# All keys and MLP rows turned by TensorE, none by transposing transfers, with a new order of operations

## The chip, the cores and the metric

One core of one Trainium2 chip runs the whole program in one launch. The time is the device time of one execution in microseconds (us). Below, PE is TensorE, DVE is VectorE, ACT is ScalarE, POOL is GpSimd and SP is the engine that here only issues transfers.

## The reference

The first half is a linear attention with a decaying state, over batch 4, 8 heads, 768 steps and a head size of 48; the second half mixes its output by a two-dimensional Fourier transform and sends it through a layer norm and an MLP from 384 to 1536 and back.

```python
for t in range(S):                                   # S = 768, D = 48
    cur = np.einsum('bhd,bhe->bhde', u[None] * kt, vt)
    y[:, :, t] = np.einsum('bhd,bhde->bhe', rt, state + cur)
    state = w[None, :, :, None] * state + np.einsum('bhd,bhe->bhde', kt, vt)
...
x = attn_out.transpose(0, 2, 1, 3).reshape(B, S, H * D)      # 4 x 768 x 384
mixed = np.real(np.fft.fft(np.fft.fft(x, axis=1), axis=2))
u = x + mixed
un = (u - mean(u)) / np.sqrt(var(u) + 1e-06)
out = u + np.maximum(un @ w_ch1, 0.0) @ w_ch2
```

Inputs r, k, v, w, u, w_ch1, w_ch2 and the output are float32.

## The kernel before

**Attention.** The sequence of each batch is cut into 6 chunks of 128 steps, 24 chunks in all (`NC`). `load` fetches k, r and v of a chunk through SP's queue. `attend` scales keys and queries by tables of the decay on DVE (`KR`, a tile of 128 steps by keys and queries of 4 pairs of heads, each padded to 128 columns) and casts v (`V`). Scores need keys and queries with the head dimension on partitions (`KRT`). For batch 0 the queries are turned once ahead of everything (`queries`, `QT6`) and the keys by 4 transposes for each chunk. For the 18 chunks of batches 1 to 3, `KRT` can be made in three ways: 8 transposes on PE into one PSUM bank (`tp`), copied out by ACT or by DVE, or one transposing transfer on SP's queue from `KR` (`xbar8`, line 468). In the kernel before, 8 of the 18 chunks take PE and 10 the transfer. Then follow the scores (line 493), the mask (`AC` on ACT with `MA` on POOL, or `MA` on DVE alone), the bonus term (`PR`, `de`, `DE`, `TT`), the carried state (`u`, `S`, `qs`) and the product with V (`y`, `X`).

**Fourier stage.** For each batch the rows are folded by symmetry (`EO`, `HH`, `XF`), then come two stages of matmuls (`fp` with `TT2` and its reversal `TR`, then `mp`), the sum `UF` with the attention's output, the centred rows `UB` and their statistics (`st`, `MV`, `rstd`).

**MLP.** The 768 rows of a batch are handled in two halves of 384, eight halves in all. The rows of a half must be turned (`UNT`), so that the model dimension is on partitions. Halves 0 and 1 do that on PE in 3 blocks (`turned`: 3 transposes, then a copy out of PSUM by DVE or ACT); halves 2 to 7 (`XBAR_HALVES`) by one transposing transfer each on SP's queue (`xbar9`, line 753). `mlp1` makes 12 tiles of 3 matmuls (line 773) with the ReLU on ACT or DVE (`HT`); `mlp2` makes 3 row blocks of 12 matmuls (line 793), a scale and sum on DVE (`osb`) and a store. W1 and W2 come by three transfers each on POOL's queue (lines 819 and 821); W2 lies in the tile that `queries` used at the start.

**What sets the order.** All operations are recorded first, each with its alternatives (engine and function), and are then emitted in an order that is written out as a list of numbers, `ORDER`. In it `468.1` is operation 468 in its second alternative, and `@4,2` names the PSUM banks it gets. Each engine runs its instructions in that order. `idle` emits a filler matmul on a tile of zeros that nothing reads; the list has 38 of them, all ahead of the first MLP matmul. Waits between engines come from the dependencies, and tiles are taken from rings in the order of emission (6 tiles of `kr`, `vt` and `KR`, 4 of `KRT`, 3 of `UNT`, 2 of `UB`).

Of the kernel before, what the change touches and what calls it, by code (L numbers as in the profile page):

```python
# [27 lines left out]
XBAR_HALVES = frozenset(range(2, 8))  # L28
# [69 lines left out]
211 182.1 188 150 173 151 157 227 171 159 180 155 176.1 229 208 160 187.1 169 167 178 168 231 174.1 158 152@0 161 181  # L98
153 185 156 205 172.1 184 170 162 179 177.1 154 165 163 233 186.1 164 235 215.1 189 196 197 200 212 201 175 216 198
218 166 199 214 190 228 213 192 295 0@1 1@1 2@1 3@1 4@1 5@1 6@1 7@1 8@1 9.1@1 219@1 194 221@2 230 217 297@3 220 313  # L100
225@4 332 315@5 222 232 223@6 351 334@7 226 298.1 353@0 316.1 236 378 224 335 299.2 317.1 10@1 11@1 12@1 13@1 14.2@1
300@1,2 303.1 234 318@5,4 319.1 193 207 210 304.1 307@6 321 301.1 380@3 237 325@1 296 322 320.1 302.1 326 308 314 15@5
16.1@5 17.2@5 305@5 239 306.1 354.1 327 355.2 18@4 19@4 20@4 356@4,2 359.1 202 333 240 309 323 360.1 363@0 328 203 357
206 310.1 248 381 324 311 352.2 364 337@4,2 340.1 336.2 312.1 358 382.2 195 238 21@7 22.2@7 383@7,6 365 341.1 344@3
379 342 345 384 386.1 338.1 390@4 249 405 329.1 330 191 346 407@6 391 242 408 209 392 343 243 183 387.1 361@5 366
362.1 339.1 385 367.1 241 347 368 409.2 331.1 388 393 430 369.1 348.1 293 349 394.1 350.1 245 370 395 389.1 371
410@7,2 413.1 411.1 250 432@6 372.1 414.1 406 415@1 412.1 396.1 244 416 204 23@0 24@0 25@0 418 417.1 373 26@0 27.1@0
419.1 486 420 433 374 28@0 29@0 30.2@0 488@0 376 397 431 246 398 421.1 448 31@2 32.2@2 440@3 489 294 400 33@2 34.1@2
450@5 399 251 377 491@7,4 404 451 375 247 422 811@2 403 823@6 423 492 424 453@1,0 254 402 441.1 425 815@5 401 428 816
449 427 812 429 819@4 426 456 820 434 821 255 813 467 824 825 814 817 822 457 826.1 252 35.1@1 36.2@1 435@1,2 438.1  # L110
487 493 439.1 469@4 818 253 442@6 1062 468 827 829@1 452 494 436.1 830.1 828 257 458 443 454 460@5 437.1 841@7 444 470
842.1 459 463 269 1061 445.1 524 861@0 831.1 867@2 1063 258 477 843.1 490 855@4 856 505 862.1 461 868.1 446 498@1 478
462 507.1@7 857 863.1 832 844 835@0 836 495 526.1@3 508.1 499 447.1 455 501 858 496@4 837 464.1 500 869.1 527.1
510@6,7 511.1 465 513 849@0 509 875@2 502.1 838 512.1 528.1 503 517@3 466.1 851@6 850 853@7 504.1 876 529@5,0 497 870
472@2,1 473.1 854 532 520 852 879@7 474.1 518 506.2 880.1 256 471.1 864 37.2@5 515 534@6 1067@5 1089@1 270 514 530.1
531.1 475 833 1068.1 1069@7 1090 859 519 521 479@0 266 1083@2 1070 834 480 877@5 533 535 516.1 522 1081@1 260 481.1
1084 1077@7 476 878.1 482 483 261 537 525 1065 541 484 1109@4 536 538 267 1079@2 1110 1131@5 1078 542.1 1125@4 1064
539 557 559.2 1129@7 485 560.2 871 1071@0 523 1072 540 263 1075@3 1132 544 1073@0 1130 545 546 1121@6 547 543 1127@5
1122 550 1117@7 632 1082 1123@6 1080 1118 548 1085@1 551 264 1074 549 1087@2 1124 552 1111@7 1128 553 272 575 1126
634@0 1086 1115@6 1076 554 1119@5 262 1088 561.1 577.1@4 259 1066 555 556 273 1112.1 881@1 882 1120.1 883 893@3 894  # L120
265 613 615.2 895 885@2 578.1 635 884 889@0 896 890 891 886 887 616.2 1097@7 888 839 562@5,1 892 580@3,4 897 563 1098
898 860 1116 1113@2 594 596.2 583 899@0 900 920@1 921 1114 579 597.2 569@6 901 581 1091@3 922 570 926@2 927 582 911@0
912 840 268 905@4 906 564 913 932@1 933 1092 558.2 928 565 584 1103@0 845 576 907 587@2 923 566 567@5 1104 846 568 847
571 572 1139@4 902 1105 588 908 651 653.2 585 590 1099 586.1 848 589 591 934 573 1100 914 872 574 617.1 1106 595 919
935 592 1107 604 1093 636.1 593 618@1,6 271 605 1094 621 274 1101 1140 929 622 654.2 1095 625@0 637@2,5 626 619 638.1
598.1 599@1,7 628 614 1145@3 1096.1 600 644@6 627 629 1141 280 940 620 640.1 639.1 602.1 641.1 603.1 623@5 1151@7
624.1 606@2 601 1161@1 1152.1 607 633 275 630 608 915 1146 645 652 631 1163@7 646 1162.1 647 648 281 642 1164 865
1167@0 668.1 643 656@1,7 649 276 669 659 657.1 609 610 655 1173@5 1168 650 660 611 1147 278 866 671 661@1 1171@0 612
662 1174 663 1102.1 664 665 658.1 1153@6 282 1155@2 1108 674 670 284 1201@5 675 1156 666 873 1193@7 1154 667 1165@2
1194 672 285 1207@6 676 1202 673 1195@1 1166 677 679 1208 1159@7 678 287 680 1169@5 681 1133@2 1170 683 279 1142 1160  # L130
682 1172 1134 903 1196 684 686.2 941@6 942 943 949@5 1148 944 721 723.2 687.2 945@7 703 946 1211@0 740 742.2 953@1
1135 288 1212.1 950 951 724.2 1136 952 702 704.2 947 954 955 948 1203@6 874 743.2 1143 956 1209@0 1149 1213@5 688 277
689@7,4 957 958.1 1204 1199@1 290 904 916 759 761.2 1210 1157@3 692 291 1197@6 1200 725.1 1137 1214 980@0 981 959@7
960 1198 286 982 992@1 993 693 1158 696@2 961 1181@5 690 283 994 965@6 966 697 962 691 909 726@0,3 745@7,4 746.1 748.1
685.2 1138.1 729 910 986@1 987 747.1 1144.1 1182 698 699 705.2 924 971@0 972 727 744.1 694@4 967 1183 695.1 988 1175@3
1150 983.1 989 733@6 712 700 749.1 734 1187@1 741.2 995 973 722.2 1176 713.1 1000 730 701 752@7 1188 968 735 1177 974
1189 917 778 780.2 753 979 731 1178 1184 732 754 936 762.2 707@0,2 736 737 706 710 755 756 1190 918 925 937 708 1185
1287@4 781.2 1179 709 1277@0 1191 714@2 728 1215@5 715 289 757 716 1299@3 1216 1186.1 758 717 718 292 1235@1 795.1
1180.1 738 750@5 1236.1 1278 1288 1300 1192.1 796.1 1291@7 739 764@0,4 765.1 711 783@3,1 784.1 766.1 767 786.1 1205@6
763.1 751.1 719 1253@0 720 760 1245@4 801.1 1254.1 1206 1251@2 975 1285@6 785.1 768 1252 769 771@0 1257@2 782 772 1246  # L140
770 773 1247@1 779 963 788@4 1258 774 775 791 964 1229@5 802 789 1292 787.1 790 792 1279@2 976 776 1297@7 1280 777
1248 793 984 1239@3 1298 797.1 794 1217@2 1286.1 1281@0 798.1 1237@1 800 1289@7 799 803 1249@4 805.1 1290 1230 1238
1283@6 1240 806 804 1295@7 807 1218 809 1296 808 1231 810 1243@1 1250.1 1001@3 1002 1284.1 1005@7 1006 1007 1244.1
1013@4 1003 1014 985 969 1015 1009@6 1232 1004.1 1016 1010 1008.1 1011 1223@1 1012 930 1219 1282 931 1017 1241@4 1018
1019@3 1020 1255@7 1021 1025@6 1026 1022.1 1031@0 1032 1027 1220 1033 1224 1028 1046@3 1047 1034.1 938 1242 1225 970
939 1023 1039 1256 1265@6 1024 1233 1052@0 1053 1226 1221 1234 1040@4 1041 1035 1301@7 1227 1271@5 990 1228.1 1266
1036 991 1222.1 1029 1259@2 996 1272 997 1042 1260 998 1030 1267 1054 1261 1044 1339@1 1048 1302 1050 1329@4 1056
1319@0 1045 1273 1320.1 1330 1043 1293@3 977 1051 1055.1 1049 1323@4 1294.1 1331@0 1060 1340.1 1324 1303 1057 1058
1335@3 1262 1336.1 1321@4 978 1274 1268 1313@1 1269 1325@3 1275 1270.1 1304 1263 1333@6 1276 1327@5 1264.1 1334 1383@2
1037 1322 1361@6 1307@4 1362.1 1384 1337@2 999 1326.1 1363@6 1338 1305 1365@3 1332.1 1308 1306 1373@2 1379@7 1314  # L150
1380.1 1371@0 1366.1 1377@7 1364.1 1349@3 1328.1 1309 1038 1369@6 1315 1370 1367@5 1374 1378 1341@6 1350 1342.1 1381@2
1375@7 1382 1355@6 1368 1372 1397@2 1356 1343@5 1310 1351 1311 1385@0 1376.1 1312.1 1316 1352 1317 1357 1353 1318.1
1398 1344 1354 1358 1399 1359 1345 1360.1 1391@4 1346 1392 1347 1386 1059 1348.1 1400 1387 1401 1393 1388 1402 1394
1389 1395 1390.1 1396.1
"""


def _order():
    out = []
    for tok in ORDER.split():  # L160
        tok, _, banks = tok.partition("@")
        n, _, a = tok.partition(".")
        out.append((int(n), int(a or 0), [int(x) for x in banks.split(",")] if banks else []))
    return out
# [3 lines left out]
def kernel(  # L168
# [11 lines left out]
    nc = tc.nc  # L180
# [8 lines left out]
    op = sch.op  # L189
# [20 lines left out]
    ident = const([128, 128], BF16, "ident")  # L210
# [441 lines left out]
    def fourier(b):  # L652
# [90 lines left out]
        for sh in range(2):  # L743
# [12 lines left out]
            else:  # L756
                for j in range(3):
                    turned(sh, j, UB, UNT)
# [102 lines left out]
```

## Time and profile before

| | |
|---|---|
| median of 3 runs | 174.62 us (173.65 to 176.54) |
| profiled execution | 176.04 us, span of its instructions 174.3 us |
| granted TensorE clock | 0.997 |
| busy PE, DVE, ACT, POOL | 160.1, 139.9, 104.5, 71.1 us |
| packets of the DMA queue that SP feeds | 89568, 22.19 MB, 65.4% of 16 engines' span |
| transposing transfers | 10 of keys and queries, 6 of MLP rows |

Rows of groups in the profile read: line, engine, operation, tiles written and read, shape and count, then busy time, mean duration in ns, and the idle time of the engine just before them with what ended it. Matmuls are pipelined: the duration of one is its latency, and the distance between starts in the timeline is what it takes of PE. Rows of waits read: who waited, for whom, us in total, how often, the longest.

### The profile page before, as it was taken

How to read it: one execution, taken by the hardware profiler on the slowest of the kernel's cores; microseconds unless marked ns; L12 is line 12 of the kernel's file. 1: busy time of each engine (PE TensorE's matmuls, PEld its weight loads, DVE VectorE, ACT ScalarE, POOL GpSimd, SP SyncE). 2: the span in 40 equal slices, each digit the busy share in tenths (PEclk: the TensorE clock that was granted, in tenths of full speed). 3: DMA queues.
4: the chain of work that ended last, by engine and by line, in shares of the span. 5: the costliest groups of instructions: out<-in, count | busy, mean ns of one | idle time of the engine just before them, and what ended most of it. 6: DMA issues, size and time to landing. Idle time of an engine off the chain costs nothing.

```text
span 174.3 us, 4274 instructions
## 1 busy us (share of the span) xinstructions
PE 160.1 (92%) x1595; PEld 110.8 (64%) x1595; DVE 139.9 (80%) x351; ACT 104.5 (60%) x248; POOL 71.1 (41%) x106
## 2 busy tenths in 40 slices
PE   4888798789999999999999998899999999999991
PEld 1384574578676787677666765567687666666550
DVE  6498999999988998889899899569989975441632
ACT  4968999799984986685657884566433050423000
POOL 8605760178962125997300596876200001100110
PEclk9999999999999999999999999999999999999998
DMA  5999798999999999999999899870001604210323
GB/s 139 289 202 207 152 220 208 239 188 212 207 168 204 172 133 220 130 209 217 230 223 154 187 246 244 120 201 4 0 0 30 177 8 104 95 45 0 125 101 137
DMA packets 91558, 26.79 MB, mean 154 GB/s; under 512 B 86977, under 2 KB 90178, under 8 KB 91538
## 3 DMA queue, kind: packets, MB, share of 16 engines
q1 hardware_dynamic: 89568, 22.19, 65.4%
q0 software_dynamic: 1440, 3.74, 10.1%
q10 hardware_dynamic: 530, 0.59, 0.9%
q8 instruction: 12, 0.20, 0.5%
q14 instruction: 8, 0.07, 0.1%
HBM read 19.77 MB, written 4.72 MB: 140 GB/s over the span
## 4 chain that ended last, share of the span: by engine, by line
PE 58%; DMA 14%; DVE 12%; issue 5%; POOL 5%; ACT 3%; SPq 1%; DVEq 0%; ACTq 0%; POOLq 0%
PE bank L773 22%; PE bank L793 21%; DMA W<-in_moe_w_ch_dram 5%; DMA HT<-in_r_dram 3%; PE bank L661 3%; DMA KRT<-KR 3%; DMA kr<-in_r_dram 3%; PE bank L700 2%; POOL TT L566 2%; PE bank L493 2%; PE bank L578 2%; DVE HH L609 2%; DVE MA L505 2%; PE bank L384 1%; DVE KR L424 1%
## 5 line engine op out<-in xcount | busy, mean ns | idle before, releaser
L773 PE MATMUL bank<-early,W 128*128 128x384 bf16 x288 | 55.0, 327 | 0.3 <-DMA W<-in_moe_w_ch_dram 0.2
L793 PE MATMUL bank<-W,HT 128*128 128x384 bf16 x288 | 54.4, 326 | 0.0
L778 ACT ACTIVATE HT<-bank 128x384 bf16<-128x384 f32 x71 | 31.1, 501 | 24.7 <-PE bank L773 24.7
L773 PEld LDWEIGHTS <-W 128*128 128x128 bf16 x288 | 30.8, 114 | 13.2 <-DMA W<-in_moe_w_ch_dram 0.5
L793 PEld LDWEIGHTS <-HT 128*128 128x128 bf16 x288 | 26.8, 98 | 14.7
L566 POOL TENSOR_TENSOR TT<-V,DE 128x384 bf16<-128x384 bf16 x22 | 19.9, 913 | 7.7 <-ACT DE L565 4.0
L502 POOL TENSOR_SCALAR_AFFINE_SELECT MA<-AC 128x512 bf16<-128x512 bf16 x25 | 16.4, 670 | 14.8 <-ACT AC L500 10.6
L800 DVE SCALAR_TENSOR_TENSOR osb<-bank,rstd,UF 128x384 f32<-128x384 f32 x24 | 13.9, 610 | 9.7 <-PE bank L793 9.6
L804 POOL DMA_DIRECT2D out_dram<-osb x7 | 3.9, 556 | 43.2 <-DVE osb L800 43.2
L424 DVE TENSOR_TENSOR KR<-kr,wtab 128x768 bf16<-128x768 f32 x18 | 18.8, 1051 | 0.9 <-DMA kr<-in_r_dram 0.9
L779 DVE TENSOR_SCALAR HT<-bank 128x384 bf16<-128x384 f32 x25 | 13.2, 550 | 7.6 <-PE bank L773 6.9
L478 POOL TENSOR_TENSOR PR<-KRT 128x512 bf16<-128x512 bf16 x9 | 10.4, 1166 | 20.3 <-DMA KRT<-KR 20.2
L500 ACT CAST AC<-bank 128x512 bf16<-128x512 f32 x25 | 14.6, 594 | 6.5 <-PE bank L493 4.2
L505 DVE TENSOR_TENSOR MA<-bank,mtri 128x512 bf16<-128x512 f32 x23 | 15.0, 677 | 0.7 <-PE bank L493 0.6
L719 ACT ACTIVATE UB<-UF,sm 128x384 bf16<-128x384 f32 x20 | 12.0, 614 | 3.3 <-DVE UF L712 3.2
L726 DVE BATCH_NORM_STATS2 st<-UF 128x6 f32<-128x384 f32 x24 | 12.9, 546 | 0.0
L586 DVE TENSOR_TENSOR X<-bank,TT 128x384 bf16<-128x384 f32 x15 | 8.3, 550 | 4.7 <-PE bank L578 4.7
L661 PE MATMUL bank<-te_t,XF 128*128 128x193 bf16 x96 | 10.4, 248 | 0.8 <-DVE XF L624 0.8
L284 PE MATMUL bank<-zero 128*128 128x512 bf16 (+2 forms) x38 | 10.5, 398 | 0.6 <-DVE PR L481 0.5
L712 DVE SCALAR_TENSOR_TENSOR UF<-bank,X 128x384 f32<-128x384 f32 x20 | 10.5, 545 | 0.7 <-PE bank L700 0.7
L669 ACT CAST TT<-bank 97x386 bf16<-97x386 f32 x13 | 7.3, 600 | 6.2 <-PE bank L661 6.1
L661 PEld LDWEIGHTS <-XF 128*128 128x128 bf16 x96 | 8.0, 98 | 2.8 <-DVE XF L624 1.4
(113 smaller groups left out, 256.1 us busy)
## 6 DMA issues: line engine op xcount, KB each, us to landing
kr<-in_k_dram SPq DMA_DIRECT2D x24, 192.0 KB, 4.3
vt<-in_v_dram SPq DMA_DIRECT2D x24, 192.0 KB, 4.1
kr<-in_r_dram SPq DMA_DIRECT2D x18, 192.0 KB, 4.6
out_dram<-osb SPq DMA_DIRECT2D x17, 192.0 KB, 2.1
W<-in_moe_w_ch_dram POOLq DMA_DIRECT2D x6, 384.0 KB, 6.1
out_dram<-osb POOLq DMA_DIRECT2D x7, 192.0 KB, 2.3
te_t<-te_c SPq DMA_DIRECT2D x1, 579.0 KB, 5.1
HT<-in_r_dram SPq DMA_DIRECT2D x1, 576.0 KB, 4.1
```

Source lines behind the costliest of these rows:

```text
L424: one(("KR", i), "DVE", "KR", lambda: nc.vector.tensor_tensor(out=KR().rearrange("t s p (a d) -> t (s p) a d", a=2)[:, :, :, 0:D], in0=kr( ...
L500: op(("AC", i, a), [("ACT", "AC", lambda: nc.scalar.copy(AC(), A_ps[a]())), ("NONE", "", None)], r=[("A", i)], w=[("AC", i, a)], new=[AC], ...
L502: op(("MA", i, a), [("POOL", "MA", lambda: nc.gpsimd.affine_select(out=MA[a](), in_=AC(), pattern=[[0, NP], [1, 128]], base=0, channel_mul ...
L505: ("DVE", "MA", lambda: nc.vector.tensor_tensor(out=MA[a](), in0=A_ps[a](), in1=mtri.unsqueeze(1).to_broadcast([128, NP, 128]), op=AluOp.m ...
L566: op(("TT", i), [(e, key, lambda g=g: g.tensor_tensor(out=TT(), in0=V(), in1=DE().unsqueeze(2).to_broadcast([128, H, D]), op=AluOp.mult)) ...
L661: nc.tensor.matmul(fp()[:, par, :], lhsT=XF()[:, par, nb, g * CH:g * CH + 128], rhs=te_t[:, g % 2, nb, par, :], start=(nb == 0 and par == ...
L726: one(("st", b, blk), "DVE", "st", lambda: nc.vector.bn_stats(out=st(), in_=UF()[:, j, :]), r=[("UF", b, blk)], new=[st], use=[UF])
L773: nc.tensor.matmul(hp(), lhsT=W1[:, dt, ft // 4 * 512:(ft // 4 + 1) * 512].rearrange("k (m j) -> k m j", j=4)[:, :, ft % 4], rhs=UNT()[:, ...
L778: op(("HT", hf, ft), [("ACT", "HT", lambda: nc.scalar.activation(out=HT()[:, ft, :], in_=hp(), func=Act.Relu, scale=-1.0)), ("DVE", "HT", ...
L779: ("DVE", "HT", lambda: nc.vector.tensor_scalar(out=HT()[:, ft, :], in0=hp(), scalar1=-1.0, scalar2=0.0, op0=AluOp.mult, op1=AluOp.max))],
L793: nc.tensor.matmul(mo(), lhsT=HT()[:, ft, j * 128:(j + 1) * 128], rhs=W2[:, ft, :], start=(ft == 0), stop=(ft == 11))
L800: one(("osb", hf, j), "DVE", "osb", lambda: nc.vector.scalar_tensor_tensor(out=osb(), in0=mo(), scalar=rstd()[:, j:j + 1], in1=UF()[:, j, ...
```

## The change

The transposing transfers are taken out. The second and third alternative of `tp` and `KRT` that led to them are gone, so all 18 chunks of batches 1 to 3 turn their keys and queries with 8 transposes on PE and a copy out of PSUM; and `XBAR_HALVES` is gone, so all eight halves go through `turned`. `ORDER` is another list: other positions, other choices of engine, other banks, 46 fillers instead of 38. The second half of the query load goes through SP's queue instead of ACT's, and nine stores instead of seven go through POOL's.

```diff
-XBAR_HALVES = frozenset(range(2, 8))
 CAST_V = frozenset()
...
 ORDER = """
-211 182.1 188 150 173 151 157 227 171 159 180 155 176.1 229 208 160 187.1 169 167 178 168 231 174.1 158 152@0 161 181
...
+150 151 173.1 211 179 185 158 160 157 228 174 161 162 181 215 183 169 164 172 227 188 180 155 152@0 153 205 163 175
...
-            op(("tp", i), [("PE", "tp8", transposes), ("PE", "tp8", transposes), ("NONE", "", None)], r=[("KR", i), "ident"],
-               w=[("tp", i)], new=[tp], uses=[[KR], [KR], []])
+            one(("tp", i), "PE", "tp8", transposes, r=[("KR", i), "ident"], new=[tp], use=[KR])
             op(("KRT", i), [("ACT", "KRT", lambda: nc.scalar.copy(KRT(), tp())),
-                            ("DVE", "KRT", lambda: nc.vector.tensor_copy(KRT(), tp())),
-                            ("SP", "xbar8", lambda: nc.sync.dma_start_transpose(
-                                out=KRT().rearrange("d s p t -> d (s p) t"), in_=KR().rearrange("t s p c -> t (s p c)")))],
-               r=[("tp", i), ("KR", i)], w=[("KRT", i)], new=[KRT], uses=[[tp], [tp], [KR]], link=("tp", i))
+                            ("DVE", "KRT", lambda: nc.vector.tensor_copy(KRT(), tp()))],
+               r=[("tp", i)], w=[("KRT", i)], new=[KRT], use=[tp])
...
-            if 2 * b + sh in XBAR_HALVES:
-                one(("UNT", b, sh), "SP", "xbar9", lambda UB=UB, UNT=UNT: nc.sync.dma_start_transpose(
-                    out=UNT().rearrange("p j c t -> p (j c) t"), in_=UB().rearrange("p j d -> p (j d)")),
-                    r=[("UB", b, sh * 3 + j) for j in range(3)], new=[UNT], use=[UB])
-            else:
-                for j in range(3):
-                    turned(sh, j, UB, UNT)
+            for j in range(3):
+                turned(sh, j, UB, UNT)
...
-        unt = [("UNT", b, sh)] if hf in XBAR_HALVES else [("UNT", b, sh, j) for j in range(3)]
+        unt = [("UNT", b, sh, j) for j in range(3)]
```

Instructions of the built programs that differ most, before and after: key and query transposes of batches 1 to 3 on PE 64 and 144; row transposes on PE 18 and 72; copies to `KRT` of these batches 8 and 18; copies to `UNT` 6 and 24; transposing transfers 16 and 0.

More of the change, by code (lines that the diff above doesn't have):

```diff
@@ L97 @@
 ORDER = """
-211 182.1 188 150 173 151 157 227 171 159 180 155 176.1 229 208 160 187.1 169 167 178 168 231 174.1 158 152@0 161 181
[L99 to L152, printed above, removed]
@@ L153 @@
-1398 1344 1354 1358 1399 1359 1345 1360.1 1391@4 1346 1392 1347 1386 1059 1348.1 1400 1387 1401 1393 1388 1402 1394
-1389 1395 1390.1 1396.1
+150 151 173.1 211 179 185 158 160 157 228 174 161 162 181 215 183 169 164 172 227 188 180 155 152@0 153 205 163 175
+171 208 170 186.1 229 165 189 182.1 198 166 233 196 177.1 197 199 159 154 167 156 168 212 231 190 296.2 201 176.1 213
+200 235 187.1 184 216 192 295 237 217 0@1 1@1 2@1 3@1 4@1 5@1 6@1 7@1 8@1 9@1 10@1 11.1@1 12.2@1 305@1 297@2 214 202
+218 232 203 219@3 194 210 313 225@4 220 221@5 351 230 315@6 332 222 353@7 207 334@0 236 226 223@3 378 206 224 298.1
@@ new lines @@
+239 405 316.1 335 240 306 317.1 13@5 14@5 15@5 16@5 17@5 318@5,4 300@3,6 299.2 354.1 301 319.1 242 18@2 19.2@2 380@2
+307@7 303 325@6 302 321.1 322.1 320.1 195 234 20@5 21.1@5 337@5,3 340.1 304 308 336.2 191 328 309 381.1 333 238 22@4
+23@4 24.1@4 25.2@4 383@4,0 314 382 310.1 338 209 243 355 386 341.1 384.1 26@2 27@2 356@2,3 326 193 323 327 311 385.1
+241 407@4 324.1 390@5 430 312.1 28@0 29.1@0 342 248 329.1 391 344@0 379 363@7 330 343 339 357.1 345 408 347 249 346
+432@1 352 409.2 406 247 30@4 31.2@4 348.1 364 433 361@4 365 392.1 358.1 366 254 362.1 415@3 387 359.1 360.1 367.1
@@ new lines @@
+331.1 32.2@1 368 448 349 250 410@1,2 413.1 411.1 350.1 414.1 369.1 450@6 244 486 393 451 394.1 388 293 395 370 488@0
+434 416 245 396.1 412.1 417 435@7,1 438.1 389.1 453@6,5 454.1 246 439.1 397.1 489 33@2 34.1@2 418 178 419.1 251 420
+371 456 398 491@2,4 372 421.1 400 431 373 452 492 35@0 36@0 37@0 38@0 39.2@0 440@7 422 468 374 423 441.1 252 375 425
+424 449 377 428 255 487 429 40@0 41@0 42@0 43@0 44.2@0 458 399 204 376 403 45@0 819@0 401.1 455.1 815@6 294 811@3 1092
+823@4 404 253 426 436 402 1093 427 812 467 256 459.1 813 816 1091 824 820 814 825 460@5 1095 260 821 505 826 817 477
@@ new lines @@
+469@1 1094 822 818.1 442@3 507@4 457 494.1 443 478 827.1 828 508.1 470 829@0 490 463 524 830.1 861@6 461 831.1 835@7
+836 462 464 841@4 842 832 837 855@1 862.1 444 843 838 856.1 526@0 495.1 844 437 867@7 868 527.1 465 857.1 849@4 471.1
+445.1 498@2 869 858 446 472@1,0 850 499 447.1 466 493 473.1 875@7 851@4 475 853@3 474.1 496@5 863.1 476 479@1 501 854
+852.1 482 876 510@0,6 513.1 500 502 480 529@3,4 530.1 511 514.1 1097@7 481 483 870 1115@6 1098.1 864 1101@0 509 1116
+484 1113@7 1102 532 503 257 877@6 512 531.1 879@4 504 1117@0 878.1 880 497.1 533 517@3 1099@2 485 258 518 1139@6 506.1
@@ new lines @@
+528 1103@4 261 839 519 525 520 521 833 515 1140 1119@1 541 266 1100 522 542 1107@6 516.1 523 547.1 1109@2 269 1104
+1145@5 1108 543 544 1110 534@3 1159@4 270 535 557 1118 1147@6 1160 537 267 1120 1149@2 845 536 538 1114 1143@0 1150
+1096 575 272 559@4 1148 539 1144 1111@1 548 560 263 540 1155@7 545 1161@2 1156 546 264 1141@6 552 1112 632 577@0 1162
+1146 1153@3 549 1142 1105@4 550 1154 551 1133@7 578 553 1121@1 561 554 634@2 259 1106 834 555 580@5,6 635 556 562@3,0
+268 613 1134 563 1122 846 840 583 265 881@4 564 859 882 885@2 565 883 886 889@0 581 893@5 262 894 594 895 884 1123 847
@@ new lines @@
+887 287 865 890 891 569@3 579 1124 892 558.1 273 1135 570 636 888 571 572 896.1 615@6 596@4 274 566 899@0 900 597
+616.1 905@2 906 848 582 901 281 1157@5 576.2 860 907 897.1 1136 598.1 871 271 911@6 912 902 1169@0 1137 1158 567@4 913
+584 1151@2 288 898.1 1125 573 617.1 1127@7 908 568 282 1170 1152 866 574 599@5,6 614 872 618@1,2 619.1 651 275 602 585
+1128 600 586 931@3 932 1126.1 914 925@5 926 620.1 603 1138.1 601 1129 595 278 927 621 937@6 938 286 933 587@2 604
+606@5 588 652 1130 589.1 609 289 939 625@1 653@3 626 928 1131 627 590 591 923@6 607 1171 654.1 608 610 919@7 592 605
@@ new lines @@
+290 1172 920 924.1 873 622 611 874 593 628 629 644@6 655.1 284 921@3 612 630 922.1 623@4 631 940 637@7,2 638.1 291
+633.2 1197@5 639.1 640 656@3,1 659.1 657.1 624.1 668 1181@7 277 658.1 645 642 646 1191@2 1182 1173 276 1198 661@1 903
+647 648 641 1183@7 934 660.1 1163@0 292 1184 649 662 643.1 1193@5 663 650 283 947@3 1189@7 929 1174 671 1203@4 670
+1132.1 945@6 669 664 665 280 946 948.1 685 949@3 1194 666 950 1164 667 1201@6 674 675.1 285 1199@5 672 676 1237@3 673
+1200 279 679 1231@1 1204 677 678 1187@5 1192 721 1202 1223@4 1190 1225@2 680 1188 1243@6 683 1224 682 1185@7 1244 681
@@ new lines @@
+1227@5 1232 684 1235@4 1228 955@6 759 1238 956 1229@1 1226 1165 1186 740 703 963@5 964 951@3 1230 1236.1 723@2 965 702
+952 959@7 960 961 686@1 909 957 742@4 687.1 724 953 1175@2 778 954.1 966 1233@5 688.1 962 1176 1234 958.1 704@1 1195@7
+705 743.1 1177 969@3 970 967.1 968 1196.1 745@5,6 748.1 689@4,1 749.1 1178 690 971 981@7 982 692 691 694@5 975@1 976
+983 695.1 995@3 996 693 1179 1166 725.1 904 977 712 726@4,7 1167 1007@2 1008 729 1217@1 930 713 1168.1 722 730 1001@0
+1002 997 1180.1 972 1205@4 744.1 910 1009 727 731 761@3 1003 978 1218 732 779.2 733@2 696@7 1245@0 984.1 734 746 935
@@ new lines @@
+735 989@5 697 1219 741 762.1 1246 1206 998 763 991@6 993@3 990 1207 992.1 936 698.1 699 780@0 915 752@5 1208 753 916
+994.1 1011 754 755 756 700 999 1265@6 760 701 747 1015@3 917 1220 1016.1 728 918 1209 757 1266 736 737 1271@7 706.1
+758 1210.1 1269@3 781.1 1272 707@6,4 973 764@5,7 710 738 795 1241@0 1221 1270 711 1211@6 765 1000 1012 1005 1010
+783@3,1 784.1 1212 785.1 766 1242 1273@7 708 739 1019@0 786 714@1 941 771@4 1213 772 767 1020 773 750@2 974 1214 751.1
+782 1279@3 768 1215 715 1004 1281@0 1006 787 1274.1 717 1216.1 1013 774 775 1280 1283@5 979 1222.1 709 1285@6 1284.1
@@ new lines @@
+716 718 1277@7 1282.1 776 942 1259@3 777 788@5 769 1278.1 1267@0 770.1 1286.1 1239@4 980 1268 1017@7 791 943 719
+1018.1 1247@2 720 789 1253@6 796 790.1 792 1307@0 801 1287@7 798 1308 944 1313@1 802 797 793 803 1260 1314 804.1 794
+1240 1323@0 1288 1248 799.1 1324.1 1321@1 800 1261 1322 805 1329@5 806 807 1309@4 809 1254 808 1262 810 1319@7 1263
+1255 1330.1 1021@0 1264 1022 1023 1025@1 1249 1024 1029@3 1026 1030 1033@5 1034 1027 1035 1317@0 1028.1 1036 1256 1037
+1320.1 1031 1250 1318.1 1275@1 1251 1311@5 1032.1 1315@7 1252 1038 1295@0 1257 1316 1301@2 1276 985 1258.1 1312 1077@3
@@ new lines @@
+1078 1065@7 1066 1045@6 1046 1039@1 1040 1289@5 1041 1302 1047 1042 1051@1 1052 1067 1296 986 1014 1043 1071@6 1072
+987 1068 1325@7 1053 1048 1303 1079 1290 1069 1304 1073 1327@1 1326.1 1059@3 1054.1 1085@6 1291 1044 1075 1086.1 1297
+1328 1074.1 988 1060.1 1061@7 1080.1 1063@6 1298 1062.1 1064 1292 1349@1 1293 1089@3 1353@7 1305 1090.1 1087@6 1310
+1070 1365@5 1350.1 1306.1 1361@3 1088 1294.1 1081 1391@2 1299 1351@4 1392 1049 1401@1 1300 1343@6 1402 1371@0 1354
+1362 1403@2 1355@1 1404.1 1405@7 1372.1 1331@3 1076 1352.1 1357@2 1055 1409@0 1358 1369@4 1410.1 1359@2 1370 1393@0
@@ L155 @@
+1366 1360.1 1367@4 1406.1 1407@5 1082 1056 1368.1 1083 1395@2 1084 1394.1 1397@7 1396 1050 1356.1 1344 1398.1 1415@4
+1408.1 1345 1411@0 1399@2 1412 1332 1400 1427@1 1057 1346 1333 1347 1363@7 1413@5 1421@0 1414 1428 1364 1379@2 1429
+1373@6 1430 1337@5 1431 1374 1058 1422 1432 1416 1348 1375 1334 1380 1335 1385@7 1381 1336 1417 1376 1382 1377 1338
+1383 1378.1 1418 1384.1 1339 1419 1386 1340 1420 1387 1341 1423 1388 1342 1424 1389 1425 1390.1 1426.1
 """
```

## The prediction

> **What bounds the kernel now.** I read the page's slices first, then busy time by stretch, then the waits of TensorE (PE) in the long stretch, then the chain that ended last and the timeline.
>
> ```profile
> PE   4888798789999999999999998899999999999991
> ...
> DVE  6498999999988998889899899569989975441632
> ```
> ```profile
> 0.00:46.60 46.60, 38.76 (x499) 26.86 (x500) 41.22 (x111) 39.81 (x91) 25.63 (x46) 1.00 1.02 206
> 46.60:135.40 88.80, 86.36 (x888) 61.87 (x885) 78.91 (x191) 57.45 (x141) 43.35 (x57) 1.00 0.86 156
> 135.40:170.10 34.70, 34.70 (x215) 22.07 (x214) 18.76 (x50) 7.29 (x18) 2.16 (x4) 1.00 0.25 80
> ```
> The columns of the second view are length, then busy time of PE, PE's weight loads, DVE, ACT and POOL, granted clock, DMA share, GB/s. There are two regimes. Up to 46.6 us (the front: attention of batch 0 and part of batch 1, Fourier stage of batch 0) PE is busy for 38.8 us, 10.5 us of it filler matmuls on a tile of zeros; DVE with 41.2 and ACT with 39.8 us set the pace. From the first MLP matmul at 46.6 to the last at 170.1 PE is busy for 86.36+34.70 = 121.1 of 123.5 us. What PE waited for there:
>
> ```profile
> PE bank L493 <- DMA KRT<-KR: 1.5, 2, 0.9
> PE bank L524 <- POOL V L434: 0.4, 1, 0.4
> PE bank L555 <- DVE osb L800: 0.2, 1, 0.2
> PE bank L773 <- DMA W<-in_moe_w_ch_dram: 0.2, 1, 0.2
> ```
> So the transposing transfers cost PE 1.5 us in all, at two places. The chain of waits (start, length, what) agrees: the first MLP matmuls wait for W1, then PE runs to the end, the last 69 matmuls at 11.23/69 = 0.163 us each.
>
> ```profile
> 39.10 8.08 DMA W<-in_moe_w_ch_dram
> ...
> 47.23 1.33 PE bank L773 x7
> ...
> 158.73 11.23 PE bank L793 x69
> ```
>
> **Part 1: turns added to PE.** The built program has no DmaTranspose left (16 before). Ten more chunks turn keys and queries with 8 TensorE transposes each (64 to 144), and six more halves turn their rows in 3 blocks of 3 (18 to 72). A matmul's row in a group is its latency, 219 ns; in a packed queue the price is the distance from start to start, which the timeline gives:
>
> ```profile
> 43.47 0.49 PE L736 MATMUL bank<-ident,UB 128*128 128x128 bf16 x6
> 43.80 0.33 PE L581 MATMUL bank<-TT,ident 128*128 128x384 bf16 x1
> ...
> 60.11 0.61 PE L462 MATMUL bank<-ident,KR 128*128 128x128 bf16 x8
> 60.56 2.21 PE L661 MATMUL bank<-te_t,XF 128*128 128x193 bf16 x24
> ```
> Eight in 0.45 us, six in 0.33: 0.056 us each. What matters is where they stand. I counted PE's instructions ahead of and behind the first MLP matmul in both built orders. Behind it the changed kernel has 80 more key turns (4.5 us) and 57 more row turns (54 new, 3 formerly ahead; 3.2 us), and by the reordering 8 more of the attention products with V (0.2), 4 of the bonus products (0.1) and 4 of the state updates (0.2), each by starts in the same timeline. That is **+8.2 us of PE work in the stretch that PE fills**. It lies beside nothing: the only cover is PE's own idle, 123.5-121.1 = 2.4 us. Ahead of the first MLP matmul there are 8 more filler matmuls (38 to 46), about 0.22 us each; they stand where PE waits for others and cost nothing while it does, and 1.7 us if it doesn't.
>
> [...]
>
> **Part 2: evictions added.** Each turn now ends in PSUM and must be copied out: ten 128x1024 copies (5 more each on ACT and DVE) and 18 of 128x384 (11 more on ACT, 7 on DVE).
>
> ```profile
> L466 ACT COPY KRT<-bank 128x1024 bf16<-128x1024 bf16 x5 | 5.2, 1050 | 0.3 <-PE bank L462 0.3
> ...
> L467 DVE COPY KRT<-bank 128x1024 bf16<-128x1024 bf16 x3 | 2.0, 676 | 0.0
> ...
> L739 DVE COPY early<-bank 128x384 bf16<-128x384 bf16 x4 | 1.2, 335 | 0.0
> ...
> L740 ACT COPY early<-bank 128x384 bf16<-128x384 bf16 x2 | 1.0, 482 | 0.0
> ```
> ACT: 5x1.05+11x0.48 = 10.6 us, under 57.5 busy of 88.8: hidden. DVE: 5x0.68+7x0.34 = 5.7 us. The new order also moves other work between engines; by counts in the middle stretch (first MLP matmul to the last second-stage Fourier product) times their rows, DVE gets 8.0 us more in all, among it 5 EO sums at 0.38 and 3 TT2 copies at 0.58, against 3 fewer masks at 0.68. DVE then has 78.9+8.0 = 86.9 us in a stretch that PE makes 88.8+6.4-1.5 = 93.7 long (6.4 of the 8.2 lie there): 93% where it had 89%. Still under PE, so at nothing; rival A says what it costs if that cover is gone.
>
> **Part 3: transfers removed.** The SP queue loses 16 issues of a median 1.6 us, some 25 us; behind them stood loads of later chunks and stores. PE regains at most what it waited for: **-1.5 us** (bounds 0, if the next late thing is the load, and -2.4, all its idle).
>
> [...]
>
> **Part 4: new waits.** A turn on PE stands in PE's queue: if DVE is late with KR or UB, every MLP matmul behind it waits. Lower bound 0: the key turns at 58.7 and 60.1 waited for nothing. Upper: PE's weight loads waited 1.6 us for KR at L462 over 8 turned chunks, mostly in the front, so 0.2 each, 2.0 for ten; and 0.1 for each added row block gives 1.8 more. The nearest rows are the two packed chunks, but DVE is fuller, so I take **+0.8** of 0 to 3.8.
>
> **Part 5: the front.** DVE's instructions listed ahead of the first MLP matmul add up to 0.7 us less than before by their rows, ACT's to 2.1 less. Against it, the second half of the query load moves from ACT's queue (issued at 0.80 us) behind one v load on SP, whose first five k issues took 6.46 us, 1.3 each: 1.8 us later at most, with the landing at 7.5 on the chain. The three W1 loads go out together with two of W2 just after the fold of batch 0, with 4.5 us less DVE work listed ahead of the last W1. These issues take POOL 5x0.57 = 2.9 us, and the masks behind them wait. I take **0** (bounds -4.5, if W1 alone gates the MLP, and +1.8).
>
> **Sum.** 8.2-1.5+0.8+0 = +7.5 us. The profiled execution took 176.04 us with a span of 174.3; the median of the runs is 174.62. On the median: **182.1 us**, 4.3% slower. My own range for this case is 178.5 to 185.
>
> **Rivals.**
> A, DVE becomes the bound. For: 89% busy already in the middle stretch, and close to full in the slices of the front, where PE waits for it. Against: after 135 us DVE has 18.8 busy of 34.7, so what it is late with can partly slide behind PE's work there. If the middle stretch can't pack DVE tighter than 89%, it becomes 86.9/0.89 = 97.6 us, 8.8 longer, and the rest of PE's work (1.8) comes on top: +10.6, so 185.2 us.
> B, not slower: the MLP starts earlier. W1 landed at 47.2 and released the first MLP matmul; issued after 4.5 us less DVE work, it could land at 42.7. Then 8.2-1.5-4.5 = +2.2, 176.8 us. It decides if the rows of half 0 are also turned by 43; against it, DVE and ACT have only 0.7 and 2.1 us less to do before that. A gain over 2% would need some 11 us out of the front, for which no row speaks.
> C, the change doesn't do what it says: some turns stay transfers or leave the packed stretch; then the time is the old one, 174.6 us. The built order shows none of either.
>
> **How the numbers follow.** The forecast has 0.62, rival A 0.17, rival B 0.16, anything faster than both (a gain that I don't see) 0.04, C 0.01. A measurement of this kernel tells about 2% from no change: 171.1 to 178.1 us. Slower holds the forecast and A, 0.79; same holds B and C, 0.17; faster 0.04. The range takes in B and A with its late waits: 177 to 187.
>
> **What would show it.** Right: PE busy from the first MLP matmul to the end, that stretch 130 to 132 us instead of 123.5, its start within 2 us of 46.6, key turns at 0.45 us for 8, no wait of L490's scores for a DMA. Wrong: a first MLP matmul before 44 us (B); several us of PE waits for DVE's KR, XF or copies between 47 and 145 (A); or turns that cost far from 0.056 us each in the packed queue.

## The result and the profile after

The changed kernel takes 183.6 us (median of 4 runs, 182.74 to 185.11) against 174.55 for the kernel before: ratio 1.0546, 95% interval 1.0437 to 1.0654. The profiled execution took 184.33 us, its span is 182.6, 8.3 more than before. Ratios here and below leave out runs that fell in a slower state of the chip; medians are over all runs of a kernel.

The slices of the page show where to look:

```profile
PE   5999988718999999999999999999999999999992
...
PEclk9999999995899999999999999999999999999999
```
PE (TensorE) has a hole in slices 8 and 9, and in slices 10 and 11 its granted clock drops to half and comes back. The view by stretch (length, busy PE, PE's weight loads, DVE, ACT, POOL, clock, DMA share, GB/s), cut at the first MLP matmul (50.9), at about the last second-stage Fourier product and at the last MLP matmul, with the stretch of the slow clock as a row of its own:

```profile
0.00:50.90 50.90, 40.50 (x484) 27.45 (x485) 40.51 (x109) 39.16 (x87) 25.24 (x46) 0.93 1.02 203
50.90:142.50 91.60, 91.60 (x1015) 68.71 (x1012) 83.28 (x206) 66.16 (x156) 38.59 (x51) 1.00 0.48 106
142.50:178.70 36.20, 36.20 (x241) 23.65 (x238) 20.28 (x58) 10.35 (x24) 3.23 (x6) 1.00 0.14 50
...
42.00:47.30 5.30, 5.30 (x36) 4.59 (x37) 1.74 (x5) 3.21 (x9) 3.91 (x5) 0.50 1.09 207
```
The front is 4.3 us longer (50.9 for 46.6). The stretch that PE fills is 4.2-4.3 us longer (91.6+36.2 = 127.8 for 123.5), and PE is busy through all of it. DMA's share there fell from 0.86 and 0.25 to 0.48 and 0.14. So the loss comes in two halves. PE's waits say what the first half is:

```profile
PE bank L697 <- DMA hid_t<-hid_c: 4.5, 1, 4.5
PE bank L298 <- DMA osb<-in_w_dram: 2.2, 1, 2.2
PE bank L658 <- DVE XF L621: 1.1, 2, 0.8
PE bank L462 <- DVE KR L424: 0.8, 3, 0.3
```
Line 697 is the second Fourier stage; it waited 4.5 us for its table `hid_t`. No row names a transfer of keys or rows any more. The chain shows the load itself, and the timeline of the two issuing queues what went out beside it:

```profile
33.44 8.47 DMA hid_t<-hid_c
41.91 0.05 issue
41.95 0.82 PE bank L697 x4
```
```profile
33.44 0.98 SPq L365 DMA_DIRECT2D hid_t<-hid_c  x1
```
```profile
33.64 1.71 POOL L811 DMA_DIRECT2D W<-in_moe_w_ch_dram  x3
35.33 1.08 POOL L813 DMA_DIRECT2D W<-in_moe_w_ch_dram  x2
```
SP issued the 288 KB table at 33.44; 0.2 us later POOL began to issue the five weight loads of 384 KB that the new order puts in a row. The table took 8.47 us to land, 3.8 in the kernel before.

The trace keeps every DMA packet, and the packets say what the two loads did to each other. The table's are the 128 of 2304 bytes on SP's queue. In the changed kernel the first packet of the weights started at 35.18 and the first of the table at 35.93; up to the table's last at 41.38, 7.9 us after its issue, 268 packets of the weights started among its 128. In the kernel before, where the table is issued 6.8 us ahead of the first weight load, its last packet ended 3.5 us after its issue, with none of the weights among them.

### The profile page after: what moved, and what is told of

Same layout as the page of the kernel before. It is cut to its first block, busy times and chain, and to the rows that moved or that the text cites. A ratio compares the mean times of both kernels' runs of the same rounds, so it can differ in the third digit from the quotient of the medians.

```text
span 182.6 us, 4547 instructions
## 1 busy us (share of the span) xinstructions
PE 168.5 (92%) x1734; PEld 119.8 (66%) x1734; DVE 145.0 (79%) x372; ACT 115.7 (63%) x266; POOL 67.1 (37%) x102
## 4 chain that ended last, share of the span: by engine, by line
PE 76%; DVE 5%; DMA 5%; issue 1%; SPq 1%; DVEq 0%
PE bank L765 26%; PE bank L785 26%; PE bank L697 5%; DMA hid_t<-hid_c 5%; PE bank L462 4%; PE bank L658 3%; PE bank L490 2%; PE bank L733 2%; PE bank L575 2%; PE bank L558 2%; DVE MA L502 2%; PE bank L521 1%; PE bank L552 1%; DVE HH L606 1%; SPq L405 1%
## 5 line engine op out<-in xcount | busy, mean ns | idle before, releaser
L785 PE MATMUL bank<-W,HT 128*128 128x384 bf16 x288 | 55.3, 326 | 0.0
L563 POOL TENSOR_TENSOR TT<-V,DE 128x384 bf16<-128x384 bf16 x20 | 17.1, 861 | 22.4 <-ACT DE L562 20.2
L499 POOL TENSOR_SCALAR_AFFINE_SELECT MA<-AC 128x512 bf16<-128x512 bf16 x28 | 18.6, 676 | 16.8 <-ACT AC L497 15.0
L796 POOL DMA_DIRECT2D out_dram<-osb x9 | 5.0, 553 | 43.1 <-DVE osb L792 26.6
L424 DVE TENSOR_TENSOR KR<-kr,wtab 128x768 bf16<-128x768 f32 x18 | 17.3, 970 | 0.5 <-DMA kr<-in_r_dram 0.5
L497 ACT CAST AC<-bank 128x512 bf16<-128x512 f32 x28 | 15.7, 595 | 2.4 <-PE bank L490 2.3
L502 DVE TENSOR_TENSOR MA<-bank,mtri 128x512 bf16<-128x512 f32 x20 | 13.3, 684 | 0.7 <-PE bank L490 0.6
L284 PE MATMUL bank<-zero 128*128 128x512 bf16 (+2 forms) x46 | 12.9, 408 | 0.5 <-DVE PR L478 0.3
L462 PE MATMUL bank<-ident,KR 128*128 128x128 bf16 x144 | 11.2, 224 | 0.8 <-DVE KR L424 0.8
L465 ACT COPY KRT<-bank 128x1024 bf16<-128x1024 bf16 x10 | 10.2, 1015 | 2.0 <-PE bank L462 1.9
```

Source lines behind the costliest of these rows:

```text
L424: one(("KR", i), "DVE", "KR", lambda: nc.vector.tensor_tensor(out=KR().rearrange("t s p (a d) -> t (s p) a d", a=2)[:, :, :, 0:D], in0=kr( ...
L462: nc.tensor.transpose(tp()[:, s, p, :], KR()[:, s, p, :], ident)
L497: op(("AC", i, a), [("ACT", "AC", lambda: nc.scalar.copy(AC(), A_ps[a]())), ("NONE", "", None)], r=[("A", i)], w=[("AC", i, a)], new=[AC], ...
L499: op(("MA", i, a), [("POOL", "MA", lambda: nc.gpsimd.affine_select(out=MA[a](), in_=AC(), pattern=[[0, NP], [1, 128]], base=0, channel_mul ...
L502: ("DVE", "MA", lambda: nc.vector.tensor_tensor(out=MA[a](), in0=A_ps[a](), in1=mtri.unsqueeze(1).to_broadcast([128, NP, 128]), op=AluOp.m ...
L563: op(("TT", i), [(e, key, lambda g=g: g.tensor_tensor(out=TT(), in0=V(), in1=DE().unsqueeze(2).to_broadcast([128, H, D]), op=AluOp.mult)) ...
```

## The experiments

Two questions. Is the front late because of that load, or is it paced by DVE and ACT and the table only comes last? And does the other half, 4.2 us, come from the work of the turns, as predicted, or from something else? In the diffs, 293 is the load of `te_t`, 294 that of `hid_t`, 1091 to 1093 are the loads of W1, 1094 to 1096 those of W2, and 829 is the first product of the second Fourier stage. All but two kernels are the changed one with the edit shown.

### The table loaded early

```diff
-... 388 293 395 370 ... 815@6 294 811@3 1092 ...
+... 388 293 294 395 370 ... 815@6 811@3 1092 ...
```


> Theory (late table): the load of hid_t, issued at 33.4 us and landing 8.47 us later, stops TensorE for 4.5 us and by that halves its clock for 6.8 us; issued right behind te_t (at about 27.5 us) it lands before 37.4. Then the first second-stage Fourier product starts at 37.5 to 38.5 us instead of 41.95, the granted clock stays at 1.00, and the first MLP matmul starts 4.5 to 7 us before 50.9, at 44 to 46.4. Time 183.6 falls to 176.5 to 179 us. Rival (the front is paced by VectorE and ScalarE, the table is only the last of several late things): the first MLP matmul stays above 49 us and the time falls by under 1.5 us.

Ratio to the kernel before 1.024 (1.0143 to 1.0337), from two runs of 178.7 and 179.1 us; the profiled one has a span of 177.0. The table, issued at 28.1, landed in 4.1 us; the second stage started at 37.5, the first MLP matmul at 45.15, and the clock stayed at 1.00. The theory holds, the rival falls: 5.8 us of the front hung on one load. Two more runs took 186.3 and 187.7 us, longer than the changed kernel; neither was profiled, so what held them up is open. The rest of this kernel is the changed one's:

```profile
45.10:173.10 128.00, 127.91 (x1255) 92.43 (x1250) 103.64 (x263) 75.89 (x180) 41.53 (x57) 1.00 0.42 97
```

### Fillers in the hole

```diff
-... 508.1 470 829@0 ...
+... 508.1 470 46@0 47@0 48@0 ... 64@0 65@0 829@0 ...
```


> Twenty more filler matmuls (0.215 us each, 4.3 us) stand ahead of the first second-stage Fourier product, where TensorE was idle for 4.5 us; hid_t still lands at about 41.9. Theory (the halved clock is a cost of its own): the granted clock stays at 1.00, the front's matmuls from 42 to 47.3 run at full speed, the first MLP matmul starts 2 to 2.7 us before 50.9, time down by 2 to 2.7 us. Rival (the slow matmuls hide behind VectorE and ScalarE): under 0.8 us.

182.23 us, ratio 1.0423 (1.0351 to 1.0495), span 179.5 against 182.6. The table did not land at 41.9 as expected: here it was issued 0.6 us ahead of the weights, and its last packet ended at 38.92. But the twenty fillers held PE until 41.39, so the second stage started only 0.6 us earlier than in the changed kernel. The two stretches now read:

```profile
37.40:42.00 4.60, 4.60 (x29) 2.37 (x27) 2.16 (x5) 1.50 (x2) 0.00 (x0) 1.00 1.09 208
42.00:47.30 5.30, 5.29 (x91) 4.62 (x89) 4.38 (x13) 5.12 (x15) 4.45 (x6) 1.00 1.09 208
```
From 42.0 to 47.3 PE did 91 matmuls where the changed kernel did 36, DVE 4.38 us of work for 1.74. The first MLP matmul came at 47.93. So the halved clock was a cost of its own: 50.90-47.93 = 3.0 us, less the 0.6 by which the second stage started earlier, some 2.4 us, about what was expected. The medians differ by 1.4 us, the ratios by 0.0123, or 2.1 us.

In the changed kernel PE went idle at 37.45, the clock fell to half at 40.43, 3.0 us later, and stayed there for 6.83 us.

### W2 behind its third load

```diff
-... 825 460@5 1095 260 ... 469@1 1094 822 ... 1150 1096 575 ...
+... 825 460@5 260 ... 469@1 822 ... 1150 1095 1094 1096 575 ...
```


> The two first W2 loads are issued with the third one, some 25 us later, so that only the three W1 loads (1.15 instead of 1.92 MB) go out beside hid_t. If the table is late because the weight loads crowd the DMA engines, it lands in 5 to 7 us instead of 8.47, the first second-stage Fourier product starts at 39 to 40.5 us, and the time falls by 1.5 to 5 us. If its place in SP's queue alone makes it late, it still lands near 41.9 and the time stays within 1 us.

185.51 us, ratio 1.0618 (1.0516 to 1.0719): no faster than the changed kernel. The table's last packet ended at 36.12, 3.5 us after its issue, and the first MLP matmul started at 44.91, but W2 is now needed before it is there:

```profile
PE bank L785 <- DMA W<-in_moe_w_ch_dram: 3.5, 1, 3.5
```
With that wait the clock was at half again, for 6.8 us (0.981 on average over the run). As a test of crowding the run says little: SP happened to issue the table at 32.6, a microsecond ahead of the weights, whose first packet started at 35.89, and that alone may have saved it.

### The weights one mask later

This run separates the two. The table keeps its place in SP's queue, all five weight loads are there, and only their issue moves by one instruction on POOL.

```diff
-... 811@3 1092 823@4 ... 402 1093 427 ... 816 1091 824 ... 1095 260 ... 469@1 1094 822 ... 457 494.1 ...
+... 811@3 823@4 ... 402 427 ... 816 824 ... 260 ... 469@1 822 ... 457 1092 1093 1091 1095 1094 494.1 ...
```


> The changed kernel with one thing moved: the five weight loads stand one mask later in POOL's queue (behind the instruction that followed them), so that they go out some 1 to 3 us later; hid_t keeps its place in SP's queue (issued at 33 to 34 us) and as many bytes are loaded. Theory (hid_t is late because the weight loads go out within 0.3 us of it and share the DMA engines with it): hid_t lands 5 to 6 us after its issue instead of 8.47, the first second-stage Fourier product starts by 39.5 us, the clock keeps 1.00, time down by 3 to 6 us. Rival (its place in SP's queue alone makes it late): landing stays above 7.5 us, the first second-stage product after 41 us, time within 1 us.

179.02 us (178.31 to 179.45, 4 runs), ratio 1.0226 (1.0151 to 1.0301). The timelines of SP and POOL:

```profile
32.85 0.80 SPq L365 DMA_DIRECT2D hid_t<-hid_c  x1
```
```profile
34.74 1.71 POOL L811 DMA_DIRECT2D W<-in_moe_w_ch_dram  x3
```
With 1.9 us between them (SP also issued the table 0.6 us earlier than in the changed kernel) the table's last packet ended at 36.41, 3.6 us after its issue, sooner than expected and ahead of the first packet of the weights at 36.88. The second stage started at 37.68, the clock stayed full (1.00 over the first 46.0 us), and the first MLP matmul started at 46.03. The same bytes are loaded, so the overlap in time is what counted here, not the place in SP's queue. The price is small: PE waits 1.0 us for W1.

### Table early, W2 in the middle

```diff
-... 388 293 395 ... 815@6 294 811@3 ... 1095 260 ... 1094 822 ... 466 493 473.1 ... 863.1 476 479@1 ...
+... 388 293 294 395 ... 815@6 811@3 ... 260 ... 822 ... 466 493 1094 473.1 ... 863.1 476 1095 479@1 ...
```


> The best form of the changed kernel that the runs point to: hid_t behind te_t, and the first two W2 loads one by one at about 47 and 50 us, after the three of W1 and before the first use of W2 at about 58 us. Theory (the front was late through crowded loads only): first MLP matmul at 43.5 to 45.5 us, the stretch behind it 127.5 to 128.5, span 175.5 to 177.5, time 1 to 2.5% above the kernel before. Rival (W2 is late again, as when it was moved behind its third load): a wait of the second MLP layer for W2 over 1 us, time above 180.

Ratio 1.0265 (1.0199 to 1.0332), four of six runs between 178.9 and 180.4 us: no better than the one-mask shift. The two longer ones took 184 to 185, and one of these was profiled. There the table is in time, but the next load that goes out with the weights, r of a later chunk at 33.6, is caught instead; its line in the chain:

```profile
33.59 10.12 DMA kr<-in_r_dram
```
PE waited 3.9 us for the keys and queries made from it, and the clock was at half for 3.4 us after it (0.990 on average over the run). That is one execution, so I take it as an example of the same thing and not as a proof. It does say that moving the table alone leaves the crowd in place.

### Key turns done twice

```diff
+                for _ in range(2 if i >= 12 else 1):
                     for s in range(2):
                         for p in range(NP):
                             nc.tensor.transpose(tp()[:, s, p, :], KR()[:, s, p, :], ident)
```


> The twelve key turns behind the first MLP matmul are each done twice into the same bank, 96 transposes more and nothing else. By the price read from the timeline, 0.056 us each on a full queue: 5.4 us longer, all of it between the first and the last MLP matmul (127.7 to 133.1 us). Rival (turns fill gaps of TensorE, or the later scores and copies hide them): under 2 us. Rival (each turn also delays its copy and so VectorE): over 8 us.

The stretch from the first to the last MLP matmul:

```profile
46.05:179.10 133.05, 133.05 (x1349) 97.69 (x1346) 103.93 (x263) 76.82 (x180) 42.49 (x57) 1.00 0.39 91
```
133.05 us against 127.8 (x1349 matmuls against 1015+241): 5.3 us for 96 transposes, 0.055 each, where 0.056 was read from the timeline. DVE's busy time did not move (103.9 against 103.6). On this full queue a turn cost its start-to-start time, no less and no more; both rivals fall. (In this run's profile the table was issued at 33.0, 1.2 us ahead of the weights; its last packet ended 3.5 us later and the front was short, 46.05 us. Nothing ahead of the first MLP matmul was edited here: the same front is late in the changed kernel's profile and short in this one, by a microsecond between two issues. The time, 185.99, ratio 1.0621 with 1.0529 to 1.0713, holds both effects.)

### The turns in the old order

This is the kernel before with its own list, in which each transposing transfer is replaced, where it stood, by the turn on PE and its copy.

```diff
-XBAR_HALVES = frozenset(range(2, 8))
+XBAR_HALVES = frozenset()
 # each key transfer n.2 in ORDER becomes: its turn (8 transposes) @bank, its copy n or n.1
 # each row transfer in ORDER becomes: turn @bank, copy, three times
```


> The turns without the new order: the list of the kernel before, in which each of the 16 transposing transfers is replaced, at its place, by the turn on TensorE and its copy (keys alternately to ScalarE and VectorE, rows 11 to ScalarE and 7 to VectorE). From the first to the last MLP matmul the kernel before takes 123.5 us. Theory (the turns cost 134 x 0.056 = 7.5 us of TensorE and buy back the 1.5 to 2 us that it waited for transfers): 129 to 130 us, time 180 to 181.5 us. Rival (it takes the new order to make the turns pack): over 132 us, time over 183. Rival (the turns find idle time by themselves): under 127.5 us, time under 178.5.

196.51 us, ratio 1.1229 (1.1178 to 1.128). The stretch took 145.4 us instead of the 129 to 130 of my theory. The rival is right: put in without retiming, the turns cost far more than their work. PE's waits, largest first (two rows of the start-up left out):

```profile
PE bank L774 <- ACT KRT L467: 3.0, 3, 1.1
PE bank L737 <- ACT early L741: 2.7, 5, 0.6
...
PE bank L525 <- DVE MA L506: 1.1, 1, 1.1
PE bank L794 <- ACT KRT L467: 1.1, 1, 1.1
```
All but the third are matmuls that need a bank or a tile that a copy has not finished with (in this kernel, lines 774 and 794 are the two MLP layers, 737 the row turns, 467 and 741 the copies of ACT); the third waits for a mask. The clock also halved once, for 3.4 us (0.991 on average over the run). Where three row turns share a bank, each waits for the copy of the one before (line 737: 7 waits, 3.5 us). The banks were my choice, so the size of this is partly mine; that a turn brings a copy on whose end PE then waits is not.

### Only the rows turned, in the old order

```diff
-XBAR_HALVES = frozenset(range(2, 8))
+XBAR_HALVES = frozenset()
 # the row transfers in ORDER are replaced as above, the key transfers stay
```


> As the run before, but only the rows of halves 2 to 7 are turned on TensorE; the ten transfers of keys stay. Theory: 54 x 0.056 = 3.0 us more on TensorE, at most 0.3 us of waits regained, stretch 126 to 126.8 us, time 177 to 178. The difference to the run before is the ten key turns: 4.5 us less 1.5 to 2 regained, 2.5 to 3 us. Rival (the transfers of keys are late because those of rows stand ahead of them in SP's queue): the waits of the scores for transfers go too, and the stretch stays at 125 us or below.

184.82 us, ratio 1.0558 (1.0518 to 1.0598), stretch 132.6 us for the expected 126 to 126.8. The same waits for copies of row turns (2.7 us on ACT's, 0.8 on DVE's) are there; both theory and rival put it too short. The rival is right in one thing: the scores no longer wait for any transfer. Keys then cost 145.4-132.6 = 12.8 us more, not 2.5 to 3.

### The transfers in the new order

The reverse: the new order with `hid_t` early, ten chunks' keys and the rows of halves 2 to 7 by transfer again, each as early as its tiles allow.

```diff
-... KR of chunk i ... tp i @bank ... KRT i ...
+... KR of chunk i, KRT i by transfer ...
-... tq, UNT three times ...
+... last UB of the half, UNT by transfer ...
```


> The new order, with hid_t loaded early, and the transfers of the kernel before put back in it: ten chunks of keys and the rows of halves 2 to 7, each issued as early as its tiles allow; their turns and copies are gone. With hid_t early alone the stretch from the first to the last MLP matmul takes 127.9 us. Theory (transfers cost TensorE waits, which the turns buy back): 127.9 - 7.5 = 120.4 us of work and 2 to 5 us of waits for transferred keys and rows, 122.5 to 125.5. Rival (the idle time that the changed kernel lost is the new order's merit alone): under 1 us of such waits, 120.5 to 121.5 us, and the time 4 us below the kernel before.

189.22 us, ratio 1.078 (1.0716 to 1.0844). PE's waits (line 493 is the scores, 773 the first MLP layer):

```profile
PE bank L493 <- DMA KRT<-KR: 7.1, 4, 4.0
PE bank L773 <- DMA early<-UB: 3.3, 3, 1.8
```
7.5 us of PE work less, and 10.4 us of waits for transfers in its place; the stretch is 137.9 us, also because the clock was at half for part of it (0.96 on average). The theory has the right sign and far too small a size. An order that is laid out for a turn of half a microsecond had no room here for a transfer, which in the kernel before took a median of 4.5 to 4.6 us from issue to landing.

### Six chunks by transfer

```diff
-... tp i @bank, KRT i ...                      # i = 15, 16, 19, 20, 22, 23
+... KRT i by transfer, near KR of chunk i ...
```


> The new order, with hid_t loaded early, and only the keys of the six chunks with 9 us or more of TensorE work between their scaling and their scores (15, 16, 19, 20, 22, 23) by transfer. Theory: 48 x 0.056 = 2.7 us less on TensorE and no wait for these transfers, stretch 125.2 us, span 174 to 175, level with the kernel before (within 1%). Rival (transfers come late even with that room, or crowd the loads): over 127 us, no gain on the run with hid_t early.

The four runs spread from 179.14 to 191.14 us, and no ratio came of them. The one at 179.14 was profiled: the stretch is 126.9 us for 127.9, so only 1.0 of the 2.7 us of turns taken away is left; the scores wait 0.5 us for a transfer, and other waits came up. Undecided as a verdict; it points to no version that beats the kernel before, and I found none.

## Why the prediction was right, and where it was wrong

The sum was +7.5 us, 182.1; the measured median is 183.6, inside the case's own range. But two of its terms were wrong in opposite directions: the waits by -3.3 us, the front by +4.3. That they nearly cancel is luck, and the forecast's own signs show it: the stretch took 127.8 us and not 130 to 132, and it started at 50.9, more than 2 us from 46.6. The other signs came: PE busy to the end, no score waiting for a DMA, turns at their price.

**Part 1, the turns: right.** +8.2 us of PE work in the packed stretch, at 0.056 us each turn; doubling measured 0.055. Part 2, the copies at nothing, held too: in that stretch PE waited for none of them.

**Parts 3 and 4, waits: mis-sized.** I took -1.5 for the transfers' waits and +0.8 for new ones, -0.7 together. The stretch grew by 4.2 us under 8.2 us of new work, so idle time fell by 4.0. Two errors made that. The bound "all its idle, 2.4" came from PE's busy time, which counts a matmul's latency (219 ns in a turn's row, for 0.056 us from start to start), so short gaps behind a matmul are hidden in it; adding up the distances between starts beyond the price of each kind gives an estimated 5.1 us of slack in the kernel before and 1.2 after (7.4 and 3.4 with the median distance of each kind as its price; the difference is the same). And the new waits were zero, not 0.8: behind 50.9 PE waited for no KR, no copy and no bank. How much of the 4.0 is due to the transfers' going (the 1.5 to 2 that named them) and how much to the tighter order stays open: every run that changed one without the other (old order with turns, new order with transfers) broke what the order had been laid out for.

**Part 5, the front: wrong, and outside its bounds.** I took 0 of -4.5 to +1.8; it was +4.3. I had seen that the five weight loads now go out in a row, but priced them only for POOL's time and for when W1 lands, not for what else was being loaded in those microseconds. Without that crowding the front comes out at 45.1 (table early) to 46.0 us (weights later) for 46.6, near the 0 that I took.

**Rivals.** A, DVE as the bound: DVE was busy for 83.3 of 91.6 us, 91%, and PE waited for it nowhere there. B, an earlier MLP: it shows only with the table out of the way, and by 1.7 us at most (44.91, with W2 late), not 4.5. What comes next there is not shown: with the table early PE, DVE and ACT were busy for 7.26, 7.32 and 7.06 of the last 7.7 us before the first MLP matmul.

So the loss has two parts. The turns' work, less what the new order packs better, is what stays when the crowding is taken away: 2.3% (ratio 1.0226, 1.0151 to 1.0301), about half of the 4.3% that the forecast took for it. The rest, up to the measured 5.5%, is a load issued at the wrong moment, and the halved clock behind it; it is not a cost of turning on TensorE.

## What to carry to other kernels

On a queue that is already full, price added matmuls by start-to-start time and expect to pay all of it (0.055 us a turn here); ask of a transfer that is taken away what anyone waited for it, since 16 transfers here had cost TensorE only a few microseconds (1.5 us in waits that name them). When an order changes, list what every queue issues within the same microseconds: here a block of large loads moved ahead delayed a small one that TensorE needed (7.9 us to its last packet with a lead of 0.2 us, 3.5 to 3.8 with leads of 1.0 to 5.6); and waits of 4.5, 3.9 and 3.5 us that TensorE had here each went with a stretch at half the clock (6.83, 3.4 and 6.8 us). An order and its means of moving data fit each other: changing one without retiming the other cost 8 to 12% here in either direction, more than the change itself.

## What the runs showed of the hardware

The table's time fell from 7.9 to 3.5 us as the lead of its issue over the weight loads' went from 0.2 to 1.0 us. By the packets of the traces:

| kernel | lead of the table's issue over the weights', us | issue to the table's last packet, us | packets of the weights among the table's |
|---|---|---|---|
| changed | 0.2 | 7.9 | 268 |
| fillers in the hole | 0.6 | 5.9 | 155 |
| W2 behind its third load | 1.0 | 3.5 | 1 |
| key turns done twice | 1.2 | 3.5 | 0 |
| weights one mask later | 1.9 | 3.6 | 0 |
| table loaded early | 5.6 | 3.8 | 0 |

The granted clock halved 3.0 us into the 4.5 us wait of the changed kernel and stayed at half for 6.83 us, though matmuls ran again: some 2.4 us more lost.

Another such stretch had no long gap ahead of it. With the key turns doubled, the clock was at half from 35.0 us on for 3.4 us although no gap of TensorE in the 5 us before was over 0.71 us; it had been busy for half of the 3.4 us before (second column):

```profile
31.60:35.00 3.40, 1.72 (x17) 1.05 (x15) 3.30 (x15) 3.33 (x7) 1.21 (x3) 1.00 1.14 217
35.00:38.40 3.40, 3.40 (x31) 3.20 (x30) 2.57 (x4) 1.79 (x4) 2.68 (x5) 0.50 1.11 248
```
With the weights one mask later TensorE was busy for 1.56 of the same 3.4 us, and the clock stayed at 1.00 in that stretch and in the next. So its busy time there does not decide alone; what does is not shown.
